# The opening of an attention kernel: where its exponentials and its scores lie, and when the first weights are split

## Chip, core and metric

The kernel runs on one core of a Trainium2 chip. What is measured is the device time of one execution, in microseconds (us), as the median of several executions. The engines are named as in the profile: PE is TensorE (matmuls; PEld are its weight loads), DVE is VectorE, ACT is ScalarE, POOL is GpSimd, and SP issues the DMAs.

## What is computed

Three layers in a row: attention with a local causal softmax and a memory term, a dense mixture of four experts, and a routed mixture of eight experts with a fixed capacity. The change concerns the first part of the attention alone.

```python
def _attn_ref(q, k, v, M_prev, z_prev, beta):       # B, H, S, D = 2, 8, 576, 64
    scores = np.where(causal, -1e9, scale * q @ k.T)
    scores = scores - scores.max(-1, keepdims=True)
    a = np.exp(scores)
    a /= a.sum(-1, keepdims=True) + 1e-09
    local = a @ v
    q_p = phi(q)                                    # phi(x) = (x if x > 0 else exp(x) - 1) + 1
    mem_out = (q_p @ M_prev) / (q_p @ z_prev + 1e-06)
    return g * mem_out + (1 - g) * local            # g = sigmoid(beta)

x = attn_out                                        # (1152, 512)
x = sum over e of p[:, e] * (relu(x @ w1[e]) @ w2[e])    # 4 experts, F = 1024
return the routed mixture of 8 experts of x
```

## The kernel before

**The opening** (function `attn0`) does the first 128 rows of all 8 heads, once for each batch b = 0, 1, as a generator in three parts whose order is written out by hand. For each b the heads go in two groups of four, x = 0 and 1, so that four groups follow each other: b0x0, b0x1, b1x0, b1x1. A group makes its scores on PE in one PSUM tile S of 128x512 (L175 to L177), takes the row maxima on DVE (L178), the exponentials on ACT, one instruction for each head (L181, with the row sums in `st`), the factor 1 / (sum * (1 + e^beta)) on DVE (L183, L184), and multiplies the exponentials by it on DVE, one instruction for each head (L187). The exponentials lie in SBUF, in the place of the keys (`kq`). The third part turns each group with four transposes (L207) into a PSUM tile T, copies T to SBUF as AT (x = 0 on DVE, L212; x = 1 on ACT, L210) and multiplies by v (L216) into X. The memory term is made beside it: `ee`, `qp` and `nm` on DVE (L188 to L194), four transposes of `qp` (L198), a copy on ACT (L200), L203 on PE. X goes to `xTh` and `xTl` (L219 on ACT, L220 on DVE), the high and low part of x that every matmul of the experts reads.

**Behind it** come eight passes of attention for the other rows, (b, hp), with names `QS`, `KH`, `KL`, `S`, `a`, `AT`, and between them the first expert's work, as PE has room: the weights come in half experts ("halves"), which `load_half` splits into a high part on ACT (L403, w1h and w2h) and a low part on POOL (L404, w1l and w2l), 8 pieces of 128x512 each. `group` multiplies 256 rows at a time: L416 to L419 are layer 1, L434 to L444 layer 2, whose PSUM tiles P are two in number. The first half is number 6: its load is issued early in the opening (`AHEAD[6]`).

The program's text is in the order of the string SCHED, but each engine's queue is set by a scheduler that places instructions as soon as what they need is there by its own estimate. `tc.issue_after(i)` keeps what stands under it behind the instruction i. Pools decide when a buffer comes free: the transfers of the second pass (kqt, L231) go into the space of the opening's tiles and start when those have been read for the last time.

Of the kernel before, what the change touches and what calls it, by code (L numbers as in the profile page):

```python
# [16 lines left out]
F32 = mybir.dt.float32  # L17
# [3 lines left out]
AF = mybir.ActivationFunctionType  # L21
OP = mybir.AluOpType
PS = bass.MemoryType.PSUM
# [9 lines left out]
def tile_kernel(ctx, tc, kq0, qv0, kqt, qvt, mbd, z_prev, beta, dprob, w1, w2, wg, u1, u2, out):  # L33
    nc = tc.nc
    B, H, D = z_prev.shape
    S = kqt.shape[3] // 4
# [16 lines left out]
    moe = ex_moe.enter_context(tc.tile_pool(name="moe", bufs=1))  # L53
# [62 lines left out]
    ex_set = ExitStack()  # L116
    sets = ex_set.enter_context(tc.tile_pool(name="set0", bufs=1, side="right", reuse_waits="tile"))
    ex_ps0 = ExitStack()
    psS = ex_ps0.enter_context(tc.tile_pool(name="psS0", bufs=2, space=PS, side="right"))
    psT = ex_ps0.enter_context(tc.tile_pool(name="psT0", bufs=4, space=PS, side="right"))  # L120
    psX = ex_ps0.enter_context(tc.tile_pool(name="psX0", bufs=2, space=PS, side="right"))

    zb = att.tile([128, B, H, D], F32, name="zb")
# [11 lines left out]
    PEI, EV = {}, {}  # L135
# [13 lines left out]
    def attn0(b):  # L149
        kq, rqv = RAW.pop(b)  # L150
# [5 lines left out]
        for x in range(2):  # L156
            hs = slice(4 * x, 4 * x + 4)
# [9 lines left out]
        st = sets.tile([128, 3, H], F32, name="st0", bufs=2)  # L167

        a = [kq[:, h // 4, 0, h % 4] for h in range(H)]
        for x in range(2):  # L170
            hs = slice(4 * x, 4 * x + 4)
            Sp = psS.tile([128, 4, 128], F32, name="S", bufs=2)
            for h in range(4):
                hh_ = 4 * x + h
                nc.tensor.matmul(Sp[:, h], QS[:, hh_], KH[:, hh_], start=(h == 0), stop=False, skip_group_check=True)  # L175
                nc.tensor.matmul(Sp[:, h], QS[:, hh_], KL[:, hh_], start=False, stop=False, skip_group_check=True)
                nc.tensor.matmul(Sp[:, h], identb, cmask, start=False, stop=(h == 3), skip_group_check=True)  # L177
            nc.vector.tensor_reduce(st[:, 0, hs], Sp, axis=X, op=OP.max, negate=True)  # L178
            for h in range(4):
                hh_ = 4 * x + h  # L180
                nc.scalar.activation(a[hh_], Sp[:, h], AF.Exp, bias=st[:, 0, hh_:hh_ + 1],  # L181
                                     accum_out=st[:, 1, hh_:hh_ + 1])
            nc.vector.scalar_tensor_tensor(st[:, 2, hs], st[:, 1, hs], 1e-9, G1[:, hs], op0=OP.add, op1=OP.mult)  # L183
            nc.vector.reciprocal(st[:, 2, hs], st[:, 2, hs])  # L184
            for h in range(4):
                hh_ = 4 * x + h
                nc.vector.tensor_scalar(a[hh_], a[hh_], st[:, 2, hh_:hh_ + 1], None, op0=OP.mult)  # L187
        nc.vector.tensor_scalar(ee, ee, 1.0, None, op0=OP.min)  # L188
        nc.vector.scalar_tensor_tensor(qp, rq, 0.0, ee, op0=OP.max, op1=OP.add)
        nc.vector.tensor_tensor(ee, qp, zb[:, b], op=OP.mult)  # L190
# [193 lines left out]
    AHEAD = {}  # L384

    def load_raw(j):
        e = j // 2
        r1 = moe.tile([128, 4, FH], F32, name="raw", bufs=2)
        nc.sync.dma_start(r1, w1[e, j % 2])
        r2 = moe.tile([128, 4, Dm], F32, name="raw", bufs=2)  # L390
        nc.sync.dma_start(r2, w2[e, j % 2])
        return r1, r2

    def load_half(j, pool, tag=""):
        r1, r2 = AHEAD.pop(j) if j in AHEAD else load_raw(j)
        W = []
        for nm_, r in (("w1", r1), ("w2", r2)):
            ch = []
            for c in range(4):
                src = r[:, c].rearrange("p (a b) -> p a b", a=4)  # L400
                hi = pool.tile([128, 4, 128], F32R, name="%sh%d%s" % (nm_, c, tag), bufs=1)
                lo = pool.tile([128, 4, 128], F32R, name="%sl%d%s" % (nm_, c, tag), bufs=1)
                nc.scalar.activation(hi, src, AF.Copy)  # L403
                nc.gpsimd.tensor_tensor(lo, src, rd(hi), op=OP.subtract)  # L404
                ch.append((hi, lo))
            W.append(ch)
        return W

    def layer1(W, xv, n, hh, hl, f_off):
        for f in range(4):  # L410
            P = psM.tile([128, 512], F32, name="P")
            wh, wl = W[0][f]
            x = 0
# [11 lines left out]
    def layer2(Ws, hh, hl, i, t, e, first, hold={}):  # L425

        Y = psM.tile([128, 512], F32, name="P")
        x, tot = 0, 12 * len(Ws)
        for g, W in enumerate(Ws):
            for f in range(4):  # L430
# [53 lines left out]
    psS = ex_att.enter_context(tc.tile_pool(name="psS", bufs=3, space=PS, side="right", reuse_waits="tile"))  # L484
    psT = ex_att.enter_context(tc.tile_pool(name="psT", bufs=2, space=PS, side="right", reuse_waits="tile"))
# [18 lines left out]
    W = None  # L504
    for op in SCHED.split():
        i = int(op[1:2] or 0)
        if op[0] == "s":
            start(i)
        elif op[0] == "f":
            if i:  # L510
                front(i)
            else:
                with tc.issue_after(EV["act"].ins), tc.issue_after(EV["dve"].ins):
                    front(i)
        elif op[0] == "n":
            next(gens[i])
        elif op[0] == "L":
            W = load_half(i, moe)
        elif op[0] == "G":
            group(i, W, *TG[op[2]])  # L520
        elif op[0] == "P":
            probs()
# [265 lines left out]
    for step in SEQ.split():  # L788
        if step[0] == "L":
            W = load_half(int(step[1]), moe)  # L790
# [610 lines left out]
```

## Time and profile before

| what | value |
|---|---|
| median of 3 runs | 800.53 us (798.32 to 801.27) |
| the profiled execution | 799.31 us |
| its span, first to last instruction | 797.5 us |
| PE busy | 737.0 us, 92% of the span |
| DVE, ACT, POOL busy | 415.2, 322.4, 360.0 us |
| mean granted clock of TensorE | 0.97 |

The profiled execution is 1.8 us longer than its span, which is what lies before the first and behind the last instruction. PE is the busiest engine over the whole span, so what matters is where it is not busy.

### The profile page before, as it was taken

The page shows a single profiled execution, that of the slowest core. Times are in us where ns is not written, and L with a number is a line of the kernel's source. Part 1 is how long each engine was busy: PE and PEld are TensorE (multiplying, and loading weights), DVE is VectorE, ACT ScalarE, POOL GpSimd, SP SyncE. Part 2 cuts the span into 40 slices and gives each one's busy share as a digit, 9 for nine tenths or more (in the row PEclk, how much of TensorE's full clock was granted, in tenths as well). Part 3 has the DMA queues.
Part 4 walks back from the last instruction along what each step waited for, and adds up shares of the span by engine and source line. Part 5 has one row for each costly group of instructions (what it writes and reads, how often), then busy time and mean ns, then how long its engine had stood idle before and what let it go on. Part 6 is the DMA issues. An engine that isn't in the chain of part 4 may idle for free.

```text
span 797.5 us, 13248 instructions
## 1 busy us (share of the span) xinstructions
PE 737.0 (92%) x5144; PEld 632.1 (79%) x5144; DVE 415.2 (52%) x1068; ACT 322.4 (40%) x761; POOL 360.0 (45%) x315
## 2 busy tenths in 40 slices
PE   5578999999999999999999999999995888899995
PEld 4466777778888878778898888998973688899995
DVE  7789576575644445543245757222968773211000
ACT  6456555563645454441143435432645212111110
POOL 1578558573654645532052337752432445432010
PEclk9799999999999999999999999999986998999999
DMA  8653345433233213212240321522100699974000
GB/s 330 241 219 124 106 166 195 159 141 134 83 106 136 106 53 130 98 67 73 80 141 26 121 106 54 210 107 81 54 28 1 241 389 404 364 291 179 16 23 23
DMA packets 25310, 111.80 MB, mean 140 GB/s; under 512 B 3560, under 2 KB 10784, under 8 KB 15136
## 3 DMA queue, kind: packets, MB, share of 16 engines
q1 hardware_dynamic: 19600, 72.69, 25.4%
q0 software_dynamic: 5648, 38.28, 12.9%
q8 instruction: 40, 0.66, 0.3%
q14 instruction: 22, 0.18, 0.1%
HBM read 106.21 MB, written 4.75 MB: 139 GB/s over the span
## 4 chain that ended last, share of the span: by engine, by line
PE 69%; issue 10%; DVE 9%; POOL 2%; DMA 1%; ACT 1%; another core or an unknown queue 0%; POOLq 0%; ACTq 0%; DVEq 0%
PE P L434 24%; PE P L416 23%; PE P L1287 4%; PE X L372 3%; PE T L363 2%; PE P L1297 2%; PE S L330 1%; PE S L299 1%; POOL out_dram L1310 1%; PE LT L627 1%; PE S L300 1%; DVE G L700 1%; PE X L350 1%; PE T L365 1%; DVE KL L256 1%
## 5 line engine op out<-in xcount | busy, mean ns | idle before, releaser
L404 POOL TENSOR_TENSOR w1l<-raw,w1h 128x512 fp32r<-128x512 f32 x88 | 116.2, 1332 | 152.6 <-ACT w1h L403 139.1
L416 PE MATMUL P<-xTh,w1h 128*128 128x256 f32 (+1 forms) x480 | 146.6, 306 | 4.9 <-DVE hl L419 4.0
L404 POOL TENSOR_TENSOR w2l<-raw,w2h 128x512 fp32r<-128x512 f32 x88 | 114.5, 1328 | 76.2 <-ACT w2h L403 72.2
L416 PE MATMUL P<-xTl,w1h 128*128 128x256 f32 (+1 forms) x480 | 143.4, 299 | 0.6 <-DVE xTl L220 0.6
L416 PE MATMUL P<-xTh,w1l 128*128 128x256 f32 (+1 forms) x480 | 143.7, 299 | 0.0
L434 PE MATMUL P<-w2h,hh 128*128 128x512 f32 x264 | 107.0, 408 | 4.9 <-DVE hl L419 4.9
L434 PE MATMUL P<-w2h,hl 128*128 128x512 f32 x264 | 104.1, 399 | 0.5 <-DVE hl L419 0.3
L434 PE MATMUL P<-w2l,hh 128*128 128x512 f32 x264 | 104.0, 396 | 0.0
L419 DVE SCALAR_TENSOR_TENSOR hl<-P,hh 128x256 fp32r<-128x256 f32 (+1 forms) x120 | 54.1, 454 | 91.8 <-ACT hh L418 91.5
L416 PEld LDWEIGHTS P<-xTh,w1h 128*128 128x128 f32 x480 | 91.3, 190 | 8.5 <-DVE hl L419 5.5
L403 ACT ACTIVATE w1h<-raw 128x512 fp32r<-128x512 f32 x88 | 54.9, 630 | 99.9 <-PE P L416 82.3
L416 PEld LDWEIGHTS P<-xTl,w1h 128*128 128x128 f32 x480 | 91.3, 190 | 2.4 <-DVE xTl L220 0.8
L416 PEld LDWEIGHTS P<-xTh,w1l 128*128 128x128 f32 x480 | 91.2, 190 | 0.5 <-issue 0.2
L444 DVE SCALAR_TENSOR_TENSOR acc<-P,pr,acc 128x512 f32<-128x512 f32 x61 | 44.5, 745 | 64.6 <-PE P L434 64.6
L1297 PE MATMUL P<-HT,ub 128*128 128x144 f32 x512 | 66.8, 288 | 3.6 <-issue 3.6
L403 ACT ACTIVATE w2h<-raw 128x512 fp32r<-128x512 f32 x88 | 53.0, 630 | 41.8 <-PE P L434 17.3
L1287 PE MATMUL P<-xg,ua 128*128 128x144 f32 x480 | 67.7, 298 | 1.5 <-DVE xg L1239 0.8
L1297 PEld LDWEIGHTS P<-HT,ub 128*128 128x128 f32 x512 | 64.1, 190 | 4.1 <-issue 4.0
L1287 PEld LDWEIGHTS P<-xg,ua 128*128 128x128 f32 x480 | 63.8, 199 | 2.6 <-DVE xg L1239 1.3
L434 PEld LDWEIGHTS P<-w2h,hh 128*128 128x128 f32 x264 | 50.2, 190 | 15.8 <-DVE hl L419 5.7
L418 ACT ACTIVATE hh<-P 128x256 fp32r<-128x256 f32 (+1 forms) x120 | 48.0, 402 | 28.4 <-PE P L416 28.0
L434 PEld LDWEIGHTS P<-w2h,hl 128*128 128x128 f32 x264 | 49.9, 189 | 11.5 <-DVE hl L419 1.4
(402 smaller groups left out, 1284.0 us busy)
## 6 DMA issues: line engine op xcount, KB each, us to landing
raw<-in_moe_w_dram SPq DMA_DIRECT2D x46, 1024.0 KB, 4.7
kqt<-in_kqt_dram SPq DMA_DIRECT2D x7, 1152.0 KB, 5.0
qvt<-in_qvt_dram SPq DMA_DIRECT2D x7, 576.0 KB, 3.7
LR<-lrd SPq DMA_DIRECT2D x7, 512.0 KB, 3.9
kq<-in_kq_dram SPq DMA_DIRECT2D x4, 512.0 KB, 3.5
x2d<-acc SPq DMA_DIRECT2D x8, 256.0 KB, 2.0
acc<-in_kqt_dram SPq DMA_DIRECT2D x1, 1152.0 KB
rqv<-in_qv_dram SPq DMA_DIRECT2D x2, 512.0 KB, 12.0
```

What stands on the lines that cost most here:

```text
L256: nc.vector.scalar_tensor_tensor(KL, kt, 0.125, rd(KH), op0=OP.mult, op1=OP.subtract)
L363: nc.tensor.transpose(Tv[:, h, o:o + 128], A[c][:, h, kb * 128:kb * 128 + kr], identf)
L372: nc.tensor.matmul(Xp[h * 64:h * 64 + 64, f0:n], rv[0:kr, kb, h], AT[0:kr, h, 0:w], start=False, stop=(kb == u[-1]), skip_group_check=True)
L403: nc.scalar.activation(hi, src, AF.Copy)
L404: nc.gpsimd.tensor_tensor(lo, src, rd(hi), op=OP.subtract)
L416: nc.tensor.matmul(P[:, 0:n], a_[:, c], xv(b_, c), start=(x == 0), stop=(x == 3 * ND - 1))
L418: nc.scalar.activation(hh[:, f_off + f, 0:n], P[:, 0:n], AF.Relu)
L419: nc.vector.scalar_tensor_tensor(hl[:, f_off + f, 0:n], P[:, 0:n], 0.0, rd(hh[:, f_off + f, 0:n]), op0=OP.max, op1=OP.subtract)
L434: m = nc.tensor.matmul(Y, a_[:, 4 * g + f, hs], b_.rearrange("p a b -> p (a b)"), start=(x == 0), stop=(x == tot - 1))
L444: EV[0] = nc.vector.scalar_tensor_tensor(acc[:, t], Y, sc, acc[:, t], op0=OP.mult, op1=OP.add)
L1287: tick(nc.tensor.matmul(P[:, s], w, g[:, c], start=(s == 0 and c == 0), stop=(s == 1 and c == ND - 1), skip_group_check=True))
L1297: tick(nc.tensor.matmul(P[:, s], ub[:, f, dd * 128:(dd + 1) * 128], HT[:, f], start=(s == 0 and f == 0), stop=(s == 1 and f == FC - 1), sk ...
```

## The change

Five edits. (1) The exponentials are written back to where the scores lay, in PSUM. (2) The four multiplications of a group become one, which reads PSUM and writes `kq`. (3) The score tiles S get four PSUM banks instead of two. (4) The transpose tiles T get two instead of four. (5) The split of half 6 stands behind the last exponential of the opening.

```diff
-    psS = ex_ps0.enter_context(tc.tile_pool(name="psS0", bufs=2, space=PS, side="right"))
-    psT = ex_ps0.enter_context(tc.tile_pool(name="psT0", bufs=4, space=PS, side="right"))
+    psS = ex_ps0.enter_context(tc.tile_pool(name="psS0", bufs=4, space=PS, side="right"))
+    psT = ex_ps0.enter_context(tc.tile_pool(name="psT0", bufs=2, space=PS, side="right"))
...
-            Sp = psS.tile([128, 4, 128], F32, name="S", bufs=2)
+            Sp = psS.tile([128, 4, 128], F32, name="S", bufs=4)
...
             for h in range(4):
                 hh_ = 4 * x + h
-                nc.scalar.activation(a[hh_], Sp[:, h], AF.Exp, bias=st[:, 0, hh_:hh_ + 1],
-                                     accum_out=st[:, 1, hh_:hh_ + 1])
+                EV["exp"] = nc.scalar.activation(Sp[:, h], Sp[:, h], AF.Exp, bias=st[:, 0, hh_:hh_ + 1],
+                                                 accum_out=st[:, 1, hh_:hh_ + 1])
...
-            for h in range(4):
-                hh_ = 4 * x + h
-                nc.vector.tensor_scalar(a[hh_], a[hh_], st[:, 2, hh_:hh_ + 1], None, op0=OP.mult)
+            nc.vector.tensor_tensor(kq[:, x, 0], Sp, st[:, 2, hs][:, :, None].to_broadcast([128, 4, 128]), op=OP.mult)
...
         elif op[0] == "L":
-            W = load_half(i, moe)
+            if i in AHEAD:
+
+                with tc.issue_after(EV["exp"].ins):
+                    W = load_half(i, moe)
+            else:
+                W = load_half(i, moe)
```

The new multiplication is L185. From there on a line of the changed kernel has a number smaller by 2 than before (L212 becomes L210).

DVE's queue in the middle of the opening, before. `st_145` and `kq_103` belong to b = 0, `st_252`, `kq_108`, `ee_212` and `qp_213` to b = 1.

```order
L187 TENSOR_SCALAR kq_103<-kq_103,st_145 128x128 x8
L194 TENSOR_TENSOR qp_142<-qp_142,nm_143 128x512
L188 TENSOR_SCALAR ee_212<-ee_212 128x512
L178 TENSOR_REDUCE st_252<-S 128x4
L183 SCALAR_TENSOR_TENSOR st_252<-st_252,G_79 128x4
L184 RECIPROCAL st_252<-st_252 128x4
L189 SCALAR_TENSOR_TENSOR qp_213<-rqv_121,ee_212 128x512
L187 TENSOR_SCALAR kq_108<-kq_108,st_252 128x128 x4
L190 TENSOR_TENSOR ee_212<-qp_213,zb 128x512
L212 COPY AT_233<-T 128x512
```

The same place of DVE's queue with the change (L192 is the old L194, L210 the old L212; b = 1 has `st_246`, `kq_108`, `ee_206`, `qp_207`):

```order
L185 TENSOR_TENSOR kq_103<-S,st_145 128x512
L192 TENSOR_TENSOR qp_142<-qp_142,nm_143 128x512
L185 TENSOR_TENSOR kq_103<-S,st_145 128x512
L178 TENSOR_REDUCE st_246<-S 128x4
L186 TENSOR_SCALAR ee_206<-ee_206 128x512
L183 SCALAR_TENSOR_TENSOR st_246<-st_246,G_79 128x4
L187 SCALAR_TENSOR_TENSOR qp_207<-rqv_121,ee_206 128x512
L184 RECIPROCAL st_246<-st_246 128x4
L210 COPY AT_227<-T 128x512
L188 TENSOR_TENSOR ee_206<-qp_207,zb 128x512
L185 TENSOR_TENSOR kq_108<-S,st_246 128x512
```

Twelve short multiplications became three long ones, and the copy AT of b0x0 moved ahead of the multiplication of b1x0 and of `ee`. Behind these rows stand, with the change, the factor of b1x1, the sum `nm`, the multiplication of b1x1 and the old L194 for b = 1.

ACT's queue at the same time, before, with what an instruction waits for (a semaphore of that engine); L181 are the exponentials of b1x0 and b1x1, `AT_221` the transposed `qp` of b = 0, `AT_244` the AT of b0x1:

```order
L181 ACTIVATE kq_108,st_252<-S,st_252 128x128 x3
L403 ACTIVATE w1h_1780<-raw 128x512 [waits DMAHW1_49]
...
L403 ACTIVATE w1h_1792<-raw 128x512
L181 ACTIVATE kq_108,st_252<-S,st_252 128x128 [waits DVE_49,Activation_49]
L181 ACTIVATE kq_108,st_252<-S,st_252 128x128
L200 ACTIVATE AT_221<-T 128x512 [waits PE_49]
L181 ACTIVATE kq_108,st_252<-S,st_252 128x128 x2
L403 ACTIVATE w2h_1796<-raw 128x512 [waits DMAHW2_49]
...
L210 ACTIVATE AT_244<-T 128x512 [waits PE_49,Activation_49]
```

And with the change (L401 is the old L403, L198 the old L200, L208 the old L210):

```order
L181 ACTIVATE S,st_246<-S,st_246 128x128 [waits Activation_49] x3
L198 ACTIVATE AT_215<-T 128x512 [waits PE_49]
L181 ACTIVATE S,st_246<-S,st_246 128x128 [waits DVE_49]
L181 ACTIVATE S,st_246<-S,st_246 128x128 [waits Activation_49] x3
L401 ACTIVATE w1h_1768<-raw 128x512 [waits DMAHW1_49]
...
L401 ACTIVATE w2h_1784<-raw 128x512 [waits DMAHW2_49]
...
L208 ACTIVATE AT_238<-T 128x512 [waits PE_49]
```

All eight pieces of the split now stand behind all exponentials, and three of the four exponentials of a group wait for an earlier instruction of their own engine. On POOL the order of the opening stays as it was. On SP the load of the second half of number 7 (L391) moved behind the four loads of passes 2 and 3 (kqt and qvt). In the passes behind the opening the scheduler places many instructions of PE, DVE and ACT a few places earlier or later than before; on ACT, `QS` and `KH` of the second pass stand ahead of the second `hh` (L418) and of the first exponentials (L308).

## Rows read from the trace of the kernel before

**Rows 1.** Busy time by stretch: engines with instruction counts, then clock granted, DMA share.
```profile
0.00:24.00 24.00, 13.89 (x68) 12.65 (x68) 18.39 (x42) 16.56 (x52) 7.83 (x13) 1.00 0.85 335
24.00:36.00 12.00, 4.37 (x26) 3.64 (x28) 8.69 (x20) 2.30 (x5) 6.57 (x6) 0.58 0.49 182
...
40.00:54.00 14.00, 9.61 (x67) 8.22 (x68) 12.71 (x17) 10.27 (x22) 13.69 (x10) 0.97 0.42 168
54.00:80.00 26.00, 22.57 (x132) 17.82 (x132) 24.12 (x44) 14.04 (x34) 18.71 (x15) 0.95 0.46 172
80.00:580.00 500.00, 494.63 (x3133) 413.83 (x3132) 268.65 (x631) 228.90 (x537) 245.40 (x213) 1.00 0.31 109
```
**Rows 2.** Timeline of PE, 18 to 41 us: start, duration, instruction, idle before it.
```profile
30.10 1.12 PE L216 MATMUL X<-AT,rqv 128*64 128x128 f32 x8 [6.45 <-DVE AT L212]
32.75 1.12 PE L198 MATMUL T<-identf,qp 128*128 128x128 f32 x4 [1.53 <-DVE qp L194]
33.66 1.92 PE L207 MATMUL T<-identf,kq 128*128 128x128 f32 x8
...
39.62 0.38 PE L416 MATMUL P<-xTh,w1h 128*128 128x256 f32 x1 [0.70 <-ACT xTh L219]
```
**Rows 3.** Timeline of DVE, 16 to 33 us.
```profile
16.96 1.62 DVE L187 TENSOR_SCALAR kq<-kq,st 128x128 f32<-128x128 f32 x8
18.50 0.68 DVE L194 TENSOR_TENSOR qp<-qp,nm 128x512 f32<-128x512 f32 x1
19.10 0.42 DVE L188 TENSOR_SCALAR ee<-ee 128x512 f32<-128x512 f32 x1
19.44 0.68 DVE L178 TENSOR_REDUCE st<-S 128x4 f32<-128x512 f32 x1
20.04 1.08 DVE L183 SCALAR_TENSOR_TENSOR st<-st,G 128x4 f32<-128x4 f32 x1
...
21.25 1.62 DVE L189 SCALAR_TENSOR_TENSOR qp<-rqv,ee 128x512 f32<-128x512 f32 x1
22.80 4.96 DVE L187 TENSOR_SCALAR kq<-kq,st 128x128 f32<-128x128 f32 x4
27.68 1.76 DVE L190 TENSOR_TENSOR ee<-qp,zb 128x512 f32<-128x512 f32 x1
29.37 0.68 DVE L212 COPY AT<-T 128x512 f32<-128x512 f32 x1
...
30.73 0.15 DVE L183 SCALAR_TENSOR_TENSOR st<-st,G 128x4 f32<-128x4 f32 x1
...
32.01 0.68 DVE L194 TENSOR_TENSOR qp<-qp,nm 128x512 f32<-128x512 f32 x1
```
**Rows 4.** Timeline of POOL, 19 to 31 us.
```profile
19.83 5.40 POOL L404 TENSOR_TENSOR w1l<-raw,w1h 128x512 fp32r<-128x512 f32 x4 [5.50 <-ACT w1h L403]
25.19 5.38 POOL L404 TENSOR_TENSOR w2l<-raw,w2h 128x512 fp32r<-128x512 f32 x4
```
**Rows 5.** Line 220: durations ns min/median/max, first and last start.
```profile
L220 DVE TENSOR_TENSOR xTl<-X,xTh x2: 680/682/684, 37.2 to 39.8; 128x512 fp32r<-128x512 f32 x2
```
**Rows 6.** Line 419, 30 to 120 us, the same columns.
```profile
L419 DVE SCALAR_TENSOR_TENSOR hl<-P,hh x14: 403/410/426, 44.7 to 116.6; 128x256 fp32r<-128x256 f32 x14
```
**Rows 7.** Timeline of ACT, 19 to 22 us.
```profile
19.07 2.19 ACT L403 ACTIVATE w1h<-raw 128x512 fp32r<-128x512 f32 x4 [0.73 <-DMA raw<-in_moe_w_dram]
21.17 0.35 ACT L181 ACTIVATE kq<-S,st 128x128 f32<-128x128 f32 x1
21.42 0.19 ACT L181 ACTIVATION_READ_ACCUMULATOR kq<-S,st 128x1 f32 x1
21.51 0.35 ACT L181 ACTIVATE kq<-S,st 128x128 f32<-128x128 f32 x1
```
**Rows 8.** Timeline of SP's queue, 35 to 36 us.
```profile
35.60 0.33 SPq L231 DMA_DIRECT2D kqt<-in_kqt_dram  x1
```
**Rows 9.** DMA issues of the page: KB each, median us from issue to landing.
```profile
kqt<-in_kqt_dram SPq DMA_DIRECT2D x7, 1152.0 KB, 5.0
```
## The prediction, made before the changed kernel ran

> **What bounds the kernel now.** I read the table of busy time by stretch first, to see where PE is not at work [rows 1]. From 80 to 580 us it is busy for 494.6 of 500 us: what starts there earlier by some time ends earlier by about that time. Between 24 and 36 us it is busy for 4.4 of 12, and between 40 and 80 us for 32.2 of 40. So the opening and what follows it are the place, and the question is what PE waits for there. The timeline of PE answers it [rows 2]: 6.45 us before L216 for DVE's copy AT (L212), then 1.53 us before the transposes of `qp` for DVE's L194. From L194's end, 32.01 + 0.68 = 32.69, to the first matmul of the experts (L416) at 39.62 runs a chain of 6.93 us through PE, ACT and DVE with no long wait.
>
> DVE's timeline shows why its rows are late [rows 3]. From 20.04 on four things take far longer than the same lines elsewhere: L183, 4 elements, 1.08 us; L189 1.62; four multiplications L187 4.96, while eight of them took 1.62 just before; L190 1.76. Together 9.42 us. POOL's timeline has the reason [rows 4]: its eight pieces of the split (L404) run from 19.83 to 25.19 + 5.38 = 30.57, 1.34 us each. L212, which reads PSUM, takes 0.68 in the same time. So what loses beside POOL are DVE's instructions on SBUF tiles, in the two-tile form (L183, L189, L190) and in the scalar form (L187), which wait for about a piece each.
>
> **The multiplication (edits 1 and 2).** No row of before is the new L185, a product of a PSUM tile and a factor in SBUF, written to SBUF. The nearest is L220, which reads X in PSUM and `xTh` in SBUF: 0.68 us for 128x512 [rows 5]. The lower bound is L188's 0.42 [rows 3], the upper the 1.76 of L190 if it did lose to POOL. I take 0.68, since L419, PSUM and SBUF too, took 403 to 426 ns in all 14 cases up to 117 us, with POOL working in much of that time [rows 6, 1]. In a row of such instructions one starts 0.60 after the other (18.50 to 19.10, [rows 3]). For b0 two of them take 1.2 us where eight took 1.6; since L194 now goes between them, the maxima of b1x1 (L178) start at 16.96 + 3 x 0.60 = 18.76 instead of 19.44: 0.7 us gained, 0 at the least if the pace were 0.8.
>
> A rule of the Trainium skill speaks against this edit ("VectorE: DVE Perf Modes", Why PSUM operands drop a tier): an fp32 operand in PSUM keeps DVE at one element a cycle, where a scalar form in SBUF may do two. By its clock of 0.96 GHz that is an estimated 0.53 us of streaming for a group instead of 0.27, and by that alone the change would lose about 1.1 us over four groups. The rows agree that L187 and L188 are the quick form, but four short ones still took 0.8 us and one long one takes 0.68.
>
> **Exponentials in place.** They stand on ACT in order, and three of each four now wait for the one before. Before, one started 0.34 us after the other (21.17, 21.51), while the read of the sum ended 0.44 after the start (21.42 + 0.19) [rows 7]. I take 0.50 for each, between 0.34 (the wait is free) and 0.57 (0.35 and 0.19 in series and a signal). That the result goes to PSUM no row shows; I take it as free and make its price a rival. L178 of b1x1 ends at 19.44; ACT first copies the transposed `qp` of b0 (transposes 1.12 us from L194's end at 18.24, a copy of 128x512 on ACT 0.6, a piece of the split being 2.19 / 4: until 20.0), then does four exponentials: 22.0. The other three groups' exponentials have slack: DVE's rows show no idle time before them.
>
> **The split behind the exponentials (edit 5).** ACT's first piece starts at 22.0 instead of 19.07, POOL 0.76 later as before (19.07 to 19.83), so at 22.8, and ends at 33.5 [rows 4, 7]. By then DVE has done, after 19.44, L188, L183, L189, L184, L212, L190, L185 of b1x0 and L183 of b1x1: 0.42 + 0.15 + 0.69 + 0.15 + 0.68 + 0.68 + 0.68 + 0.15 = 3.6 less some 0.08 of overlap each, so at 22.4, just free of POOL (L183 alone is 0.15). The four rows of 9.42 us become 0.15 + 0.69 + 0.68 + 0.68 = 2.2: 7.2 us gained.
>
> What is late next: behind them stand `nm`'s sum (0.67, as L178), its factor (two SBUF tiles, beside POOL now), the multiplication of b1x1, three small ones and L194, which before ran alone. I give the factor 1.0 instead of 0.15 (as L183, [rows 3]) and L194 1.7 instead of 0.68 (as L189 and L190): 1.9 us given back. From 22.4: 0.67 + 0.3 to 23.3, factor to 24.1, L185 to 24.8, small ones to 25.1, L194 to 26.8. Before it ended at 32.69, so 5.9 us are gained there (0.7 + 7.2 - 1.9, less 0.1). Bounds: 6.9 if L194 finds POOL between two pieces, 4.5 if it misses one more piece.
>
> The Trainium skill ("SBUF — State Buffer", Who interferes with whom) says that DVE with two SBUF inputs, or in its two-port form, and POOL take one port pair in turn, each for a whole instruction, and that DVE with one SBUF input does not contend. By it L185 is free of POOL and L194 waits for one piece: the same sum. Rows 3, 4 and 6 agree.
>
> **The banks (edits 3 and 4).** Four S banks let PE score b1x0 before the exponentials of b0x0 are done; DVE was behind then, so nothing comes of it. With two T banks a transpose waits for the copy two tiles earlier: that of b0x1 on ACT stands behind all eight pieces (22.0 + 8 x 0.55 = 26.4, copy to 27.0), and PE needs it only behind the transposes of `qp` at 26.8 + 1.1. For the chain from L194 to L416 I keep 6.9 us; its bounds are 5.9 (PE multiplies b0x1 while ACT copies) and 7.9 (two copies of 0.6 no longer overlapped). L416 then starts at 33.7 instead of 39.62.
>
> **Behind the opening.** Loads of the second pass start when the transposes of `kq` are done, 35.60 before, at 33.66 + 1.92 [rows 8, 2], so here near 30.6, and land 5.0 us later [rows 9] at 35.6. ACT, which now has that pass's QS ahead of the second `hh`, has the first pass's QS and KH, a piece and the first `hh` to do after L416 starts at 33.7, which I take for more than 1.9 us: no wait. The later load of half 7 has 14 us of other PE work in front of it. DVE has the same work as before after L416, so I let the whole gain through.
>
> **Sum.** The profiled execution took 799.31 us (1.8 around its span). Less 5.9 is 793.4. The median of the runs stands 1.2 above it: **794.6 us**, 0.7% faster.
>
> **Rivals.** *Given back behind the opening.* DVE is busy for 12.7 of 14 us from 40 to 54 and for 24.1 of 26 up to 80 [rows 1], and the new order puts the second pass's KL ahead of the second `hl`, for which PE needs a P tile. KL has 1152 columns, over twice L190's 512; two waits of 2 us for it (an estimate from L190's 1.76 beside POOL) leave 2 us of gain: 798.6. For it speaks that DVE, not PE, sets the pace there; against it that before `hl` stood behind as much.
>
> *POOL keeps the port.* If L194 comes through only when the eight pieces are done, at 33.5 + 0.7 = 34.2, the chain starts 1.5 us later than before: 802.0. It decides from an end of L194 at 32.7. Against it: L189, L190 and L187 each came through between pieces.
>
> *The exponentials are dear in place.* All 16 stand in a row on ACT from 10.7 to 22. With c us more for each than I take, the gain is gone at c = 5.9 / 16 = 0.37; at c = 0.65, double their length, the time is 794.6 + 10.4 = 805.0, slower. No row of before writes PSUM from ACT, so only its small price elsewhere speaks against it. The skill ("ScalarE: Activation LUTs", Step-by-step) says that PSUM is ACT's quicker destination; no run here shows it.
>
> *More.* PE's granted clock was 0.58 from 24 to 36 us [rows 1], half speed for most of it. With the wait of 6.45 us gone it may stay up, and the chain could be 3 us shorter: 791.6.
>
> **Chances.** Forecast 0.61, more 0.07, given back 0.20, port 0.05, exponentials 0.07. Half a per cent (4.0 us) is about what a measurement of this kernel can tell from no change: faster 0.68, within it 0.25, slower 0.07. The forecast's own bounds are gains of 3.5 (4.5 less 1.0) to 7.9 (6.9 and 1.0): 792.6 to 797.0. The range takes in the two neighbours, "more" and "given back", with 1 us for the spread of the runs: **790.5 to 799.6**.
>
> **What would show it.** In the changed profile: L178 of b1x1 at 18.8; POOL's first piece at 22.8 with DVE's L189 and L190 at 0.7 us; L185 at 0.68; the exponentials 0.5 apart; L194 (there L192) ending at 26.8; L416 (there L414) at 33.7; PE's idle time from 40 to 80 us unchanged when counted from that start. Wrong if L194 is later than 29, if L185 is over 1 us, or if the time from the first L416 to the first L434 grows by more than 2 us.

## The result, and the profile of the changed kernel

The changed kernel took **792.73 us** in the median of 5 runs (791.77 to 795.48), the kernel before 799.65 in 5 runs (the three of the table above among them): ratio **0.9914**, with a 95% interval from 0.9896 to 0.9932. Measured once more (E12), on a chip where the kernel before took 788.03, it was 0.9928 [0.9905, 0.9952]. So it is faster by 0.7 to 0.9%, where 0.7% was forecast (794.6). The trace below is of the execution of 795.42 us, with a mean granted clock of 0.969; three of the five took 791.77 to 792.73 us, at 0.977 to 0.980.

The timeline of DVE after, in the place of [rows 3] (a line number is smaller by 2 from the old L188 on):

```profile
18.06 0.68 DVE L178 TENSOR_REDUCE st<-S 128x4 f32<-128x512 f32 x1
...
19.17 0.69 DVE L187 SCALAR_TENSOR_TENSOR qp<-rqv,ee 128x512 f32<-128x512 f32 x1
...
20.44 0.68 DVE L188 TENSOR_TENSOR ee<-qp,zb 128x512 f32<-128x512 f32 x1
21.04 0.69 DVE L185 TENSOR_TENSOR kq<-S,st 128x512 f32<-128x512 f32 x1
21.64 0.15 DVE L183 SCALAR_TENSOR_TENSOR st<-st,G 128x4 f32<-128x4 f32 x1
21.71 0.68 DVE L189 TENSOR_REDUCE nm<-ee 128x8 f32<-128x512 f32 x1
...
22.47 0.65 DVE L190 SCALAR_TENSOR_TENSOR nm<-nm,G 128x8 f32<-128x8 f32 x1
23.04 0.68 DVE L185 TENSOR_TENSOR kq<-S,st 128x512 f32<-128x512 f32 x1
23.64 0.71 DVE L109 TENSOR_SCALAR sp<-sp 128x9 f32<-128x9 f32 x1
...
24.51 1.58 DVE L192 TENSOR_TENSOR qp<-qp,nm 128x512 f32<-128x512 f32 x1
```

POOL and then ACT at the same time, in the place of [rows 4] and [rows 7]:

```profile
21.82 5.40 POOL L402 TENSOR_TENSOR w1l<-raw,w1h 128x512 fp32r<-128x512 f32 x4 [8.77 <-ACT w1h L401]
27.18 4.95 POOL L402 TENSOR_TENSOR w2l<-raw,w2h 128x512 fp32r<-128x512 f32 x4
```

```profile
20.22 0.34 ACT L181 ACTIVATE S<-S,st 128x128 f32<-128x128 f32 x1
20.48 0.19 ACT L181 ACTIVATION_READ_ACCUMULATOR S<-S,st 128x1 f32 x1
20.71 0.34 ACT L181 ACTIVATE S<-S,st 128x128 f32<-128x128 f32 x1
20.98 0.19 ACT L181 ACTIVATION_READ_ACCUMULATOR S<-S,st 128x1 f32 x1
21.07 2.18 ACT L401 ACTIVATE w1h<-raw 128x512 fp32r<-128x512 f32 x4
```

The 4.96, 1.62 and 1.76 us of [rows 3] are 0.69, 0.69 and 0.68, all before POOL's first piece at 21.82. What now runs beside the split is the multiplication of b1x1 (0.68, untouched), two instructions on 8 and 9 elements (0.65 and 0.71) and L192 (1.58). L192 ends at 26.09; the old L194 ended at 32.69.

PE after, in the place of [rows 2]:

```profile
26.24 0.63 PE L196 MATMUL T<-identf,qp 128*128 128x128 f32 x4 [2.85 <-DVE qp L192]
...
33.07 0.38 PE L414 MATMUL P<-xTh,w1h 128*128 128x256 f32 x1 [0.70 <-ACT xTh L217]
```

The two waits of 6.45 and 1.53 us became one of 2.85, and the experts start at 33.07 instead of 39.62, 6.55 us earlier. The table by stretch, in the place of [rows 1], has PE at work for 8.29 us between 24 and 36 instead of 4.37, and hardly changed from 80 to 580 (495.19 against 494.63):

```profile
24.00:36.00 12.00, 8.29 (x54) 7.04 (x55) 7.13 (x11) 6.81 (x11) 10.57 (x9) 0.78 0.61 206
40.00:54.00 14.00, 10.93 (x55) 8.46 (x54) 13.04 (x24) 7.01 (x20) 10.94 (x8) 0.88 0.73 277
54.00:80.00 26.00, 23.39 (x147) 18.10 (x146) 22.69 (x39) 15.09 (x36) 17.83 (x13) 1.00 0.36 130
80.00:580.00 500.00, 495.19 (x3143) 414.03 (x3141) 263.80 (x629) 226.94 (x535) 242.22 (x213) 1.00 0.31 107
```

How much of the 6.55 us arrives is read from the last matmul of the same line, before and after (one line's instructions: shortest, median and longest in ns, then first and last start):

```profile
L416 PE MATMUL P<-xTh,w1h x480: 274/283/522, 39.6 to 575.1; 128*128 128x256 f32 x116, 128*128 128x384 f32 x44
```

```profile
L414 PE MATMUL P<-xTh,w1h x480: 277/283/562, 33.1 to 569.3; 128*128 128x256 f32 x116, 128*128 128x384 f32 x44
```

5.8 us arrive 530 us later; 0.7 are given back on the way.

### The profile page after: what moved, and what is told of

Its sections match the earlier page's. It is cut to its first block, busy times and chain, and to the rows that moved or that the text cites. A ratio compares the mean times of both kernels' runs of the same rounds, so it can differ in the third digit from the quotient of the medians.

```text
span 793.6 us, 13241 instructions
## 1 busy us (share of the span) xinstructions
PE 739.1 (93%) x5144; PEld 633.8 (80%) x5144; DVE 407.5 (51%) x1056; ACT 322.3 (41%) x761; POOL 357.9 (45%) x315
## 4 chain that ended last, share of the span: by engine, by line
PE 72%; issue 11%; DVE 10%; ACT 2%; POOL 1%; another core or an unknown queue 0%; DMA 0%; POOLq 0%; DVEq 0%; ACTq 0%
PE P L432 25%; PE P L414 24%; PE P L1290 4%; PE X L370 3%; PE P L1300 3%; PE T L361 2%; PE S L328 1%; PE S L297 1%; POOL out_dram L1313 1%; PE LT L630 1%; PE S L298 1%; DVE G L703 1%; PE X L348 1%; PE T L363 1%; DVE KL L254 1%
## 5 line engine op out<-in xcount | busy, mean ns | idle before, releaser
L414 PE MATMUL P<-xTh,w1h 128*128 128x256 f32 (+1 forms) x480 | 147.9, 309 | 5.0 <-DVE hl L417 4.1
L414 PE MATMUL P<-xTl,w1h 128*128 128x256 f32 (+1 forms) x480 | 144.6, 301 | 0.6 <-DVE xTl L218 0.6
L414 PE MATMUL P<-xTh,w1l 128*128 128x256 f32 (+1 forms) x480 | 144.2, 301 | 0.0
L432 PE MATMUL P<-w2h,hh 128*128 128x512 f32 x264 | 106.7, 407 | 3.7 <-DVE hl L417 3.7
L432 PE MATMUL P<-w2h,hl 128*128 128x512 f32 x264 | 104.1, 399 | 0.3 <-DVE hl L417 0.3
L432 PE MATMUL P<-w2l,hh 128*128 128x512 f32 x264 | 104.0, 396 | 0.0
L414 PEld LDWEIGHTS P<-xTh,w1h 128*128 128x128 f32 x480 | 92.1, 192 | 9.7 <-DVE hl L417 6.6
L414 PEld LDWEIGHTS P<-xTl,w1h 128*128 128x128 f32 x480 | 92.1, 192 | 2.4 <-DVE xTl L218 0.8
L401 ACT ACTIVATE w1h<-raw 128x512 fp32r<-128x512 f32 x88 | 54.9, 630 | 96.2 <-PE P L414 83.0
L414 PEld LDWEIGHTS P<-xTh,w1l 128*128 128x128 f32 x480 | 91.9, 192 | 0.7 <-issue 0.5
L401 ACT ACTIVATE w2h<-raw 128x512 fp32r<-128x512 f32 x88 | 53.1, 629 | 37.0 <-PE P L432 20.1
L432 PEld LDWEIGHTS P<-w2h,hh 128*128 128x128 f32 x264 | 50.2, 190 | 14.2 <-DVE hl L417 4.6
L416 ACT ACTIVATE hh<-P 128x256 fp32r<-128x256 f32 (+1 forms) x120 | 48.0, 402 | 30.6 <-PE P L414 30.3
L432 PEld LDWEIGHTS P<-w2h,hl 128*128 128x128 f32 x264 | 49.9, 189 | 11.0 <-DVE hl L417 0.7
```

The costliest lines, as they stand in the source:

```text
L414: nc.tensor.matmul(P[:, 0:n], a_[:, c], xv(b_, c), start=(x == 0), stop=(x == 3 * ND - 1))
L416: nc.scalar.activation(hh[:, f_off + f, 0:n], P[:, 0:n], AF.Relu)
L432: m = nc.tensor.matmul(Y, a_[:, 4 * g + f, hs], b_.rearrange("p a b -> p (a b)"), start=(x == 0), stop=(x == tot - 1))
```

## Experiments

They ran on three chips; that of the two traces above is not on record. A ratio is to the kernel before on the same chip (in groups of kernels that shared its runs: E1, E2, E3, E5 with 795.29 us; E6 to E9 with 800.37; E10 to E13 with 788.03). Their traces begin a little earlier: the changed kernel itself has its first L414 at 32.23 in E12 and at 33.07 above, so times of different traces compare to about 0.8 us. "Lost" is what DVE's instructions take longer beside POOL than the same lines elsewhere, summed from the split's start to the end of the old L194 of b1. For before it is 1.08 - 0.15, 1.62 - 0.69, 4.96 - 0.87 and 1.76 - 0.68, together 7.0 [rows 3] (0.87 is E1's uncontended row below).

| | kernel | ratio, 95% | POOL's split | lost on DVE | old L194 of b1 ends | first and last start of L416 (or the line that became of it) |
|---|---|---|---|---|---|---|
| | before | 1 | 19.83 to 30.57 | 7.0 | 32.69 | 39.6, 575.1 |
| | the change, edits 1 to 5 | 0.9914 [0.9896, 0.9932] | 21.82 to 32.13 | 1.9 | 26.09 | 33.1, 569.3 |
| E1 | edit 5 alone | 1.0030 [1.0004, 1.0056] | 22.32 to 32.62 | 6.3 | 31.48 | 39.1, 578.1 |
| E7 | edits 3 and 4 alone | 1.0003 [0.9986, 1.0019] | 18.29 to 28.91 | 7.6 | 32.56 | 39.2, 575.4 |
| E10 | one product, in SBUF, alone | 0.9992 [0.9972, 1.0012] | 18.22 to 29.42 | 6.6 | 29.97 | 37.2, 573.4 |
| E2 | edits 1 to 4 | 0.9913 [0.9885, 0.9941] | 19.34 to 30.12 | 2.8 | 25.30 | 34.3, 569.3 |
| E6 | edits 1 and 2 | 0.9882 [0.9853, 0.9911] | 18.38 to 29.60 | 2.6 | 26.02 | 36.0, 569.3 |
| E13 | edits 1 and 2, again | 0.9910 [0.9884, 0.9937] | 18.28 to 29.53 | 2.6 | 25.91 | 34.2, 568.3 |
| E12 | the change, again | 0.9928 [0.9905, 0.9952] | 21.01 to 31.34 | 1.9 | 25.29 | 32.2, 567.5 |
| E8 | the change, product in SBUF | 0.9903 [0.9871, 0.9935] | 20.93 to 31.84 | 2.8 | 27.02 | 32.4, 567.9 |
| E9 | the change, four products from PSUM | 0.9926 [0.9899, 0.9953] | 21.68 to 32.02 | 2.1 | 27.21 | 35.2, 570.1 |
| E3 | edits 1, 2 and 5 | 1.0019 [0.9996, 1.0042] | 26.00 to 36.03 | 0 | 24.24 | 34.7, 575.4 |
| E5 | the change, split later still | 0.9921 [0.9896, 0.9945] | 23.43 to 33.96 | 0 | 23.21 | 31.2, 567.4 |
| E11 | before, split later still | 0.9939 [0.9916, 0.9962] | 25.52 to 37.18 | 0 | 25.29 | 32.2, 570.9 |

**E1, the split's place alone.** The kernel before with edit 5 (the first line names the exponential that the split waits for).

```diff
-                nc.scalar.activation(a[hh_], Sp[:, h], AF.Exp, bias=st[:, 0, hh_:hh_ + 1],
+                EV["exp"] = nc.scalar.activation(a[hh_], Sp[:, h], AF.Exp, bias=st[:, 0, hh_:hh_ + 1],
...
-            W = load_half(i, moe)
+            if i in AHEAD:
+                with tc.issue_after(EV["exp"].ins):
+                    W = load_half(i, moe)
+            else:
+                W = load_half(i, moe)
```

> Edit 5 alone: exponentials and scaling as before, two S banks, four T banks, but the split of half 6 stands behind the last exponential. If the split's place is what pays (7.2 us of DVE's rows no longer beside POOL), L194 of b1 ends 5 us or more earlier than 32.69 and the time falls to 794 or less. If it only moves the waiting, the four short multiplications of b1x1 (L187) and L194 now fall beside POOL and take some 5 and 1.7 us: L194 ends at 31.5 to 33 and the time stays within 2 us of before.

It gains nothing: 1.003, 2.9 us above before, where the second of the two expectations allowed 2. DVE's timeline of E1:

```profile
20.46 0.87 DVE L187 TENSOR_SCALAR kq<-kq,st 128x128 f32<-128x128 f32 x4
21.25 0.69 DVE L190 TENSOR_TENSOR ee<-qp,zb 128x512 f32<-128x512 f32 x1
...
22.45 1.17 DVE L183 SCALAR_TENSOR_TENSOR st<-st,G 128x4 f32<-128x4 f32 x1
...
24.32 0.53 DVE L109 TENSOR_SCALAR sp<-sp 128x9 f32<-128x9 f32 x1
...
24.84 4.96 DVE L187 TENSOR_SCALAR kq<-kq,st 128x128 f32<-128x128 f32 x4
...
29.94 1.54 DVE L194 TENSOR_TENSOR qp<-qp,nm 128x512 f32<-128x512 f32 x1
```

The four rows that the prediction meant to free are free (four multiplications in 0.87). But the multiplications of b1x1, which ran alone before, now take the same 4.96 us: 7.0 us taken away, 1.02 + 0.37 + 4.09 + 0.85 = 6.3 us put back. Behind the opening it then needs 539.0 us from the first L416 to the last, where before took 535.5. The busy time of that stretch says in what (the columns of [rows 1]: length, PE, PEld, DVE, ACT, POOL busy, clock granted, DMA), of before, of E1 and of E12:

```profile
39.62:575.12 535.50, 522.31 (x3293) 436.23 (x3294) 300.98 (x676) 250.43 (x586) 277.81 (x236) 1.00 0.32 115
39.14:578.14 539.00, 525.54 (x3292) 439.94 (x3293) 298.06 (x676) 249.78 (x586) 278.10 (x236) 0.99 0.33 116
32.23:567.53 535.30, 522.74 (x3293) 435.70 (x3294) 298.04 (x676) 250.30 (x586) 276.96 (x236) 1.00 0.34 118
```

PE is idle for 13.5 us of it in E1 and for 13.2 before; of the 3.5 us more, 3.2 are spent at work, on the same matmuls. The granted clock is lower: 0.85 from 60 to 80 us and 0.91 from 120 to 160, where before had 1.00. PE had waited longer there, for DVE's `hl`, 2.09 us at 66.70 and 3.35 at 136.13 (1.88 was before's longest from 60 to 150). It is not this execution alone: the mean clock is 0.964 in the median of E1's 12 runs, 0.971 in that of before's 23. What in the order of E1 makes those waits was not tried.

**E2, the change without edit 5.** The split is issued as before.

```diff
-            if i in AHEAD:
-                with tc.issue_after(EV["exp"].ins):
-                    W = load_half(i, moe)
-            else:
-                W = load_half(i, moe)
+            W = load_half(i, moe)
```

> Edits 1 to 4 without edit 5: the scheduler places the split among the exponentials again. If the split's place is what pays, L189 and L190 (here L187, L188) take 1.6 to 1.8 us beside POOL and 2 to 3 us of the gain are lost: about 795.5. If the multiplication that reads PSUM is what pays, since it does not wait for POOL, L194 (here L192) of b1 ends within 1 us of the changed kernel's 26.09 and the time is 792 to 794.

The whole gain is there without edit 5: 0.9913. POOL starts at 19.34, the old L190 loses 1.05 (1.73 us), a product on 8 elements 1.00, the old L194 0.80, and all L185 take 0.68, two of them beside POOL.

**E3, two banks for S.** The change without edits 3 and 4.

```diff
-    psS = ex_ps0.enter_context(tc.tile_pool(name="psS0", bufs=4, space=PS, side="right"))
-    psT = ex_ps0.enter_context(tc.tile_pool(name="psT0", bufs=2, space=PS, side="right"))
+    psS = ex_ps0.enter_context(tc.tile_pool(name="psS0", bufs=2, space=PS, side="right"))
+    psT = ex_ps0.enter_context(tc.tile_pool(name="psT0", bufs=4, space=PS, side="right"))
-            Sp = psS.tile([128, 4, 128], F32, name="S", bufs=4)
+            Sp = psS.tile([128, 4, 128], F32, name="S", bufs=2)
```

> Edits 1, 2 and 5 with the banks of before (two for S, four for T). If the four S banks carry part of the gain, PE's scores of b1 wait until a bank has been scaled, L178 of b1x1 starts at 21 instead of 18.06, and the time is 2 us or more above the changed kernel: 795 or more. If nothing comes of the banks, as the prediction had it, the later exponentials are covered: 791.5 to 794.

All is lost: 1.0019. PE's timeline of E3 shows where it begins:

```profile
15.59 0.44 PE L175 MATMUL S<-KH,QS 128*128 128x128 f32 x1 [4.38 <-DVE kq L185]
```

With the exponentials in PSUM, a bank is held until the multiplication has read it, so PE may score b1x0 only then. The maxima of b1x1 come at 22.00 (18.06 with four banks), the last exponential at 24.89, and the split, which by edit 5 stands behind it, starts on POOL at 26.00. No DVE instruction loses ahead of L192, which ends at 24.24, but the first L414 starts only 10.4 us later, at 34.67 (7.0 in the change): ACT's pieces of the split now stand ahead of its copy of the transposed `qp` (L198), whose transposes PE began at 24.30.

```profile
27.32 2.18 ACT L401 ACTIVATE w2h<-raw 128x512 fp32r<-128x512 f32 x4
29.40 0.58 ACT L198 ACTIVATE AT<-T 128x512 f32<-128x512 f32 x1
```

POOL's part ends at 36.03, and from the first L414 to the last it takes 540.7 us, against 536.2 and 535.3 in the two traces of the change. Again most of that is PE at work under a lower clock: busy for 527.1 us, with a clock of 0.98. In the median of 12 runs the mean clock is 0.966.

**E7, the banks alone.** The kernel before with edits 3 and 4: the diff of E3 the other way round.

> Edits 3 and 4 alone: four S banks and two T banks, exponentials in SBUF and four multiplications for each group as before. If the banks only make room for the PSUM multiplication, L187 of b1x0 still takes some 5 us beside POOL and the ratio to before is 0.998 to 1.002. Rival: the banks carry gain of their own, since the maxima of b1 come earlier: L178 of b1x1 starts 0.7 us earlier and the ratio is 0.997 or less.

Nothing: 1.0003, and the four L187 take 4.94 us.

**E6 and E13, edits 1 and 2 alone.** The kernel before, exponentials in place, one multiplication.

```diff
-                nc.scalar.activation(a[hh_], Sp[:, h], AF.Exp, bias=st[:, 0, hh_:hh_ + 1],
+                EV["exp"] = nc.scalar.activation(Sp[:, h], Sp[:, h], AF.Exp, bias=st[:, 0, hh_:hh_ + 1],
...
-            for h in range(4):
-                hh_ = 4 * x + h
-                nc.vector.tensor_scalar(a[hh_], a[hh_], st[:, 2, hh_:hh_ + 1], None, op0=OP.mult)
+            nc.vector.tensor_tensor(kq[:, x, 0], Sp, st[:, 2, hs][:, :, None].to_broadcast([128, 4, 128]), op=OP.mult)
```

> Edits 1 and 2 alone: exponentials in PSUM and one multiplication per group, with the banks of before and the split where the scheduler puts it. If the four S banks are what the multiplication in PSUM needs (it holds its bank until DVE has scaled it, so PE scores b1 4.4 us later), nothing is gained: a ratio to before of 0.997 to 1.003. Rival: what cost the run with two S banks and the late split was that the split then began at 25 us; with the split free again L416 (here L414) starts near 34 and the ratio is 0.992 to 0.995.

These two edits give all of the gain, with the split where it was: 0.9882, and 0.9910 the second time. DVE's timeline of E6:

```profile
19.10 1.10 DVE L187 SCALAR_TENSOR_TENSOR qp<-rqv,ee 128x512 f32<-128x512 f32 x1 [0.16 <-PE T L196]
...
20.73 1.16 DVE L188 TENSOR_TENSOR ee<-qp,zb 128x512 f32<-128x512 f32 x1
...
23.21 1.06 DVE L190 SCALAR_TENSOR_TENSOR nm<-nm,G 128x8 f32<-128x8 f32 x1
...
24.54 1.48 DVE L192 TENSOR_TENSOR qp<-qp,nm 128x512 f32<-128x512 f32 x1
...
28.65 0.69 DVE L185 TENSOR_TENSOR kq<-S,st 128x512 f32<-128x512 f32 x1
```

The four with two operands in SBUF lose 0.4 to 0.9 us each; the multiplication reads PSUM and loses nothing, and since two banks let PE score b1x0 and b1x1 late, the factors (L183) and multiplications of b1 stand behind L192. The first L414 is therefore 10 us behind L192's end, at 36.0, and yet the last comes as early as in the change: from the first to the last PE is idle for 8.7 us, where before it was for 13.2. Where it waits less was not followed up. E3 differs from E6 by edit 5 alone, which holds the split back until those late exponentials, and loses all.

**E12, the change once more beside it.** No edit.

> The changed kernel once more, beside the others on this chip: 0.9914 as first measured, between 0.9896 and 0.9932.

> Edits 1 and 2 alone once more, with the change on the same chip. If edits 3, 4 and 5 cost something, it is 2 to 3 us faster than the change again (0.988 against 0.991); if its earlier 0.9882 was the spread of the runs, the two agree within 1.5 us.

E12 took 782.66 us (780.14 to 783.08), E13 780.36 (777.20 to 782.18): 2.3 us apart, as the first expectation had it. But the two ranges overlap, and E13's last L414 is not earlier (568.3 against 567.5); what differs lies in the layers behind it, which no edit touches (213.8 and 210.1 us to the end of the span). That two edits are faster than all five is therefore not shown.

**E8, one product in SBUF; E9, four products from PSUM.** Both are the change otherwise; E8 puts the exponentials back into SBUF.

```diff
# E8
-                EV["exp"] = nc.scalar.activation(Sp[:, h], Sp[:, h], AF.Exp, bias=st[:, 0, hh_:hh_ + 1],
+                EV["exp"] = nc.scalar.activation(a[hh_], Sp[:, h], AF.Exp, bias=st[:, 0, hh_:hh_ + 1],
...
-            nc.vector.tensor_tensor(kq[:, x, 0], Sp, st[:, 2, hs][:, :, None].to_broadcast([128, 4, 128]), op=OP.mult)
+            nc.vector.tensor_tensor(kq[:, x, 0], kq[:, x, 0], st[:, 2, hs][:, :, None].to_broadcast([128, 4, 128]), op=OP.mult)
# E9
-            nc.vector.tensor_tensor(kq[:, x, 0], Sp, st[:, 2, hs][:, :, None].to_broadcast([128, 4, 128]), op=OP.mult)
+            for h in range(4):
+                hh_ = 4 * x + h
+                nc.vector.tensor_scalar(a[hh_], Sp[:, h], st[:, 2, hh_:hh_ + 1], None, op0=OP.mult)
```

> The change with exponentials in SBUF: one multiplication for each group, but with both operands in SBUF; banks and the place of the split as in the change. If what counts is that the multiplication does not wait for POOL, that of b1x1 takes 1.5 to 1.8 us instead of 0.68, L194 (here L192) ends 1 us later than with the change, and the ratio to before is 0.9925 to 0.995. If what counts is that one instruction waits for one piece where four waited for four, the ratio is that of the change, 0.9914 within 0.001.

> The change with four multiplications for each group, each reading PSUM; all else as in the change. If it is the operand in PSUM that counts, each takes some 0.3 us, also beside POOL, 16 of them cost 2 us more than the four of the change on DVE, and the ratio to before is 0.992 to 0.995. If it is the joining of four into one that counts, they wait for POOL as L187 did (1.2 us each for b1x1) and the ratio is 0.996 or more.

Both keep the gain (0.9903 and 0.9926). Of E8's two expectations the row bears out the first (1.77 us); the interval of its ratio takes in both. DVE's rows of b1x1's multiplication beside POOL, of E8 and then of E9:

```profile
23.57 1.77 DVE L185 TENSOR_TENSOR kq<-kq,st 128x512 f32<-128x512 f32 x1
```

```profile
24.21 1.11 DVE L187 TENSOR_SCALAR kq<-S,st 128x128 f32<-128x128 f32 x4
```

One product from SBUF loses 1.09 us, most of a piece (1.34), four from PSUM lose nothing (1.12 beside no split, 1.11 here). With edit 5 in place either is enough; four from SBUF, E1, are not.

**E10, one product in SBUF, nothing else.** The kernel before, its four multiplications joined.

```diff
-            for h in range(4):
-                hh_ = 4 * x + h
-                nc.vector.tensor_scalar(a[hh_], a[hh_], st[:, 2, hh_:hh_ + 1], None, op0=OP.mult)
+            nc.vector.tensor_tensor(kq[:, x, 0], kq[:, x, 0], st[:, 2, hs][:, :, None].to_broadcast([128, 4, 128]), op=OP.mult)
```

> The kernel before with one edit: the four multiplications of a group become one, in SBUF on both sides; exponentials, banks and the split stay as before. My theory: what cost most was four short SBUF instructions, each waiting for a piece of the split. One long one waits for one piece, so it takes about 1.8 us beside POOL instead of 4.96; L183 (1.1), the old L189 and L190 (1.6 to 1.8) still wait. The old L194 then ends about 2.5 to 3.5 us earlier and may itself meet POOL (1.5): ratio 0.995 to 0.998. Rival A: the number of DVE instructions is all that matters, and this alone gives the whole gain: 0.991 or less. Rival B: reading PSUM is what matters, a form with SBUF on both sides loses as much: 1.000.

My theory expected 0.995 to 0.998; the ratio is 0.9992, outside of that, though its interval reaches down to 0.9972. DVE's timeline of E10:

```profile
18.83 0.69 DVE L183 SCALAR_TENSOR_TENSOR st<-st,G 128x4 f32<-128x4 f32 x1
...
19.64 1.63 DVE L187 SCALAR_TENSOR_TENSOR qp<-rqv,ee 128x512 f32<-128x512 f32 x1
21.20 1.76 DVE L185 TENSOR_TENSOR kq<-kq,st 128x512 f32<-128x512 f32 x1
22.88 1.75 DVE L188 TENSOR_TENSOR ee<-qp,zb 128x512 f32<-128x512 f32 x1
...
25.86 1.14 DVE L190 SCALAR_TENSOR_TENSOR nm<-nm,G 128x8 f32<-128x8 f32 x1
...
27.00 1.22 DVE L183 SCALAR_TENSOR_TENSOR st<-st,G 128x4 f32<-128x4 f32 x1
...
28.37 1.60 DVE L192 TENSOR_TENSOR qp<-qp,nm 128x512 f32<-128x512 f32 x1
```

The product costs 1.76 instead of 4.96, as expected. But the 3.2 us saved bring L190, the second L183 and L192 into the time of the split, where before they ran behind it (0.15, 0.15 and 0.68). They lose 0.98 + 1.07 + 0.92 = 3.0 us: the wait is handed on, and 6.6 of 7.0 us stay. The old L194 does end 2.7 us earlier than before, as expected, but up to 0.8 of that is how the traces begin, and the multiplication of b1x1 (30.00) now stands behind it; the last L414 is 1.7 us earlier. That is Rival B's number by another mechanism.

**E5 and E11, the split behind the old L194 of b1.** E5 is the change, E11 the kernel before; in both POOL's first piece waits for that instruction.

```diff
-        nc.vector.tensor_tensor(qp, qp, nm[:, :, None].to_broadcast([128, H, D]), op=OP.mult)
+        EV["qp"] = nc.vector.tensor_tensor(qp, qp, nm[:, :, None].to_broadcast([128, H, D]), op=OP.mult)
...
+        after = EV["qp"] if j in AHEAD else None
...
-                nc.gpsimd.tensor_tensor(lo, src, rd(hi), op=OP.subtract)
+                lo_i = nc.gpsimd.tensor_tensor(lo, src, rd(hi), op=OP.subtract)
+                if after is not None:
+                    tc.add_manual_dep(lo_i.ins, after.ins.name, mybir.DependencyInfo(
+                        mybir.DependencyClass.Sync, mybir.DependencyReason.DATA), reason="split behind qp")
```

> The change, with POOL's part of the split held back further, until DVE's L194 (here L192) of b1 is done. If POOL costs the opening what the prediction gave back (1.9 us), the factor of nm takes 0.16 instead of 0.65, L109 0.16 instead of 0.71, L192 0.68 instead of 1.58, so L192 ends near 24.1 instead of 26.09, L416 (here L418) starts 1.5 to 2 us earlier than 33.07 and the time is near 791. Rival: POOL's eight pieces then end near 35.5 instead of 32.13, the first pass's QS waits behind them, and what is gained before L416 is lost after it: 792.5 to 795.

> The kernel before, its four short multiplications, exponentials and banks untouched, with one thing added: the first piece of the split on POOL waits until the old L194 of b1 has been done. My theory (the multiplications are dear only beside POOL): four of them take 0.87 us for both groups of b1, L183 0.15, the old L189 and L190 0.7, the old L194 ends before 25, the first L416 starts 6 to 8 us earlier, and behind it some 2 to 4 us are lost again beside the late split: ratio 0.991 to 0.996. Rival: the four short multiplications are dear by themselves, the old L194 ends at 28 or later and the ratio stays above 0.997.

Nothing is lost ahead of the old L194. E11, whose arithmetic is word for word that of before, gains 0.6% (0.9939); so the short multiplications are dear beside POOL only. ACT's pieces stay among the exponentials (the last ends at 23.96), ahead of the copy that they hold up in E3. DVE's timeline of E11:

```profile
23.82 0.87 DVE L187 TENSOR_SCALAR kq<-kq,st 128x128 f32<-128x128 f32 x4
24.60 0.69 DVE L194 TENSOR_TENSOR qp<-qp,nm 128x512 f32<-128x512 f32 x1
...
32.02 1.64 DVE L263 SCALAR_TENSOR_TENSOR qp<-acc,ee 128x512 f32<-128x512 f32 x1
33.59 0.68 DVE L220 TENSOR_TENSOR xTl<-X,xTh 128x512 fp32r<-128x512 f32 x1
34.33 1.70 DVE L256 SCALAR_TENSOR_TENSOR KL<-acc,KH 128x1152 fp32r<-128x1152 f32 x1
```

The split is then still at work when the first pass of attention begins: L263 (L261 in the changed kernel) loses 0.95 us, and `xTl` (L220), for which PE's second matmul of the experts waits 1.70 us, stands behind it. E5 starts the experts 1 us earlier than E12 and has the last of them at the same time (567.4 against 567.5). So the 1.9 us that the change still loses were not had by moving the split later.

## Why the prediction was right, and in which step it was not

**The cause of the stall** was right: DVE's instructions on SBUF tiles lost 7.0 us beside POOL's split. E11 takes the split away from them and nothing else, and they lose 0. By the Trainium skill ("SBUF — State Buffer", Who interferes with whom) those with two SBUF inputs and `tensor_scalar` in its two-port form contend, and reductions and readers of PSUM don't. The traces agree: of the kernel after, beside the split, L190 takes 0.65 and L109 0.71, L189 (a reduction) 0.68 and L185 0.68.

**The step that failed** is the one under "The split behind the exponentials (edit 5)", the sentence "The four rows of 9.42 us become 0.15 + 0.69 + 0.68 + 0.68 = 2.2: 7.2 us gained". As a sum it was right: after, the four rows take 0.16, 0.69, 0.69 and 0.68. But it put all of it down to edit 5 and counted the multiplication at 0.7 us for b0 only. E1 and E6 show the reverse: edit 5 alone gives nothing, edits 1 and 2 alone give all. 4.1 of the 7.0 us lay in four short instructions that lose about 1 us each, and moved behind the exponentials the split still meets one of b1's two groups. The prediction listed "the multiplication of b1x1" as 0.68 among what comes behind, without asking what its old form would have cost there: 4.96.

**The banks**, "nothing comes of it", held for edits 3 and 4 alone (E7) and beside edits 1 and 2 (E2 against E6). With edits 1 and 5 both in place it failed: without four banks the split starts 4 us later, ACT's part of it stands ahead of the copy of `qp`, and the gain is gone (E3). DVE was behind, as the prediction said, but the last exponential, on which edit 5 hangs the split, was not looked at.

**The terms.** The multiplication was forecast at 0.68 and took 0.68 or 0.69, beside POOL too. One product from PSUM takes 0.68 where four from SBUF take 0.87 with no split beside them (E1), so it gains a little even there; by the rule of the Trainium skill ("VectorE: DVE Perf Modes", Why PSUM operands drop a tier) alone it would have lost. The exponentials were forecast 0.50 apart and are 0.49 (20.22 to 20.71). The result in PSUM costs nothing: 0.34 against 0.35 [rows 7]. The loss beside the late split was forecast as 1.9 us, 0.85 at the factor of `nm` and 1.0 at the old L194. They lost 0.48 (L190) and 0.90; another 0.55 went at L109, one of the "small ones" that the prediction gave no loss. That the sum is 1.9 again is luck. L183 of b1x1 came through at 21.64, just ahead of POOL, as forecast.

**Too late by 0.7 us**: L178 of b1x1 came at 18.06, not 18.76, and all that follows shifted with it: ACT's first piece 21.07 (22.0), POOL's 21.82 (22.8), L192's end 26.09 (26.8), L414 33.07 (33.7). The cause lies ahead of the stretch that the prediction looked at. With the exponentials waiting for each other, ACT takes `QS` of b1 between those of b0, so POOL's second L159 starts 1.18 us earlier and a KL on DVE (L161) no longer runs beside it (L188 does instead, and takes 1.04 us where 0.68 were enough before). On ACT, E2, E6 and E9 have that order too; E1, E7 and E8, with the exponentials in SBUF, have not. Of before and of after, POOL and DVE:

```profile
12.78 1.55 POOL L159 TENSOR_TENSOR QS<-kq,QS 64x512 fp32r<-64x512 f32 x1 [1.32 <-ACT QS L158]
...
13.26 1.63 DVE L161 SCALAR_TENSOR_TENSOR KL<-kq,KH 128x512 fp32r<-128x512 f32 x1
```

```profile
11.60 1.45 POOL L159 TENSOR_TENSOR QS<-kq,QS 64x512 fp32r<-64x512 f32 x1 [0.23 <-ACT QS L158]
...
13.52 0.68 DVE L161 SCALAR_TENSOR_TENSOR KL<-kq,KH 128x512 fp32r<-128x512 f32 x1
```

**Chain and rest.** From L192's end to L414 it took 6.98 us (6.9 forecast). "I let the whole gain through" held: of 6.55 us at the first L414, 5.8 are there at the last, though from the first L414 to the first L432 it took 15.0 us instead of 14.1. The 0.7 us are not the kernel's: in E12 it needs 535.3 us from the first to the last matmul of that line, before 535.5. In the trace above PE is busy for 525.1 us of that stretch, in E12 for 522.7, on the same matmuls, and the clock is 0.99 against 1.00. So the rival "given back" did not come. Of the other kernels' 533.3 to 540.7 us, the longest, E1, E3 and E11, have PE at work for 2.4 to 4.7 us longer than before, and idle for at most 0.8 longer. "More" did not come: the granted clock from 24 to 36 us rose from 0.58 to 0.78, and the chain is no shorter. "POOL keeps the port" did not come: L192 went through 6 us before the split's end. With 5.8 to 6.6 us gained in place of 5.9, the time of 794.6 is met within 2 us, 0.9 of which lie in the kernel before (800.53 in three runs, 799.65 in five). The two profiled executions are only 3.9 us apart: behind the last matmul of that line the one before needs 222.4 us and the one after 224.3, in the layers that no edit touches.

## What to carry to other kernels

Where one engine's instructions wait for another's pieces, count them, not their length: four short ones lost 4.1 us beside pieces of 1.34, and shortening some only brings the next ones into the same stretch (E10) unless the chain leaves it. Moving the disturbing work helps if it clears all of the chain (in E3 its part on another engine stood in front of the chain's next step), so ask of every instruction behind the one freed what it will cost beside the work in its new place (E1). And a buffer that is held longer (here a PSUM bank, until the product has read it) delays whatever is hung on its last user (E3).

## What the runs showed of the hardware that was not expected

The size of a contended instruction hardly matters: a product on 8 elements took 0.17 us in E5, where no split ran yet, 0.65 in the change and 1.14 in E10, and 512 elements lost about as much (0.4 to 1.1). One right behind another that has just waited can come through free: in E1 the product on 8 elements takes 0.15 behind L109's 0.53, in E2 L109 takes 0.16 behind L190's 1.16. The same kernel granted PE different clocks in two executions just behind the same wait: after the opening of the trace above L414 took 0.41 us each (half speed, 1.2 GHz) from 34.45 to 37.2 us, and 0.28 (2.4 GHz) from 33.44 on in E12. PE had waited 2.85 and 3.00 us for L192 a few us earlier, so this wait alone does not tell which; both traces need 15.0 us from the first L414 to the first L432. The price shows over the whole line, with all its stretches at half speed: PE is busy for 2.4 us longer in the first trace, and 0.9 of them are left from the first matmul to the last.
